# Attention block on one core: the durations and latencies in the kernel's own planner are replaced, and the first key mask is computed ahead of an evacuation

## The chip, the core and the metric

The kernel runs on one core of a Trainium2 chip. The metric is the device time of one execution in microseconds, the median of three runs. Five engines take part, each with its own instruction queue, worked off in order: PE (TensorE, matmuls), ACT (ScalarE), DVE (VectorE), POOL (GpSimd) and SP (SyncE, which here only issues DMAs).

## The reference

The inputs are x of 1 x 2048 x 448, wqkv of 448 x 1344 and wo of 448 x 448, all bf16. There are 16 heads of width 28.

```
qkv = (x @ wqkv).reshape(B, S, 3, H, Dh).transpose(2, 0, 3, 1, 4)
q, k, v = qkv[0], qkv[1], qkv[2]
scores = einsum("bhqd,bhkd->bhqk", q, k) * (Dh ** -0.5)
p = softmax(scores, axis=-1)
o = einsum("bhqk,bhkd->bhqd", p, v)
return o.transpose(0, 2, 1, 3).reshape(B, S, D) @ wo
```

## The kernel before, in words

**Tiles.** The 16 heads are four groups of four heads, the 2048 queries four column blocks of 512, and the 2048 keys 16 rows of 128. A window is one group with one block of queries: 16 windows, each with 16 rows of keys times four heads, 64 score tiles of 128 keys x 512 queries. The first two windows are cut: their rows 0 to 3 come first, then the other rows of each.

**What happens to a score tile.** A score tile is one matmul of KB (keys) and QB (queries) into PSUM (L868, `emit_S`). The extra rows in KB and QB carry an upper bound of the score, so that the exponential cannot overflow: NK (L580 for the first group, L619 for the others) is the key side of this bound, made from the maximum of the absolute keys (KPART, KMAX), and SP copies it into KB with DMAs (L595, L617). The keys themselves are evacuated from PSUM into KB (L544, L553, L561) and moved between KB's partitions by DMAs (L585, L607). From the score tile the exponential is taken in one of three ways:

- ACT: two tiles lie side by side in one of the two PSUM tiles PA, and one ACTIVATE Exp of 128 x 1024 writes PTA (L1291).
- DVE with GpSimd: the tile lies in one of three PSUM banks PD. DVE computes DU from it (L1072), then DV from it and DU (L1075); GpSimd multiplies the two into DG (L1078); DVE adds it to the tile in PSUM and writes PTD (L1091), which frees the bank. So a tile takes three passes of DVE and one of GpSimd.
- GpSimd alone: DVE copies the tile from PD to SG (L1004), and GpSimd does six operations (L1011 to L1034) that end in PTD.

When all four heads of a row are there, four matmuls add the row to PO (L1136). After a window's last row DVE copies PO to OSB (L939 and L953 for the cut windows, L956), the sums go through DRAM and come back as reciprocals, GpSimd multiplies (L971), and after the last group the output projection follows (L792, L810). In PE's spare time stand the projections for Q (L656), K (L525) and V (L727) of the next group and, where nothing else is to be done, matmuls of zeros that keep PE active (L1252).

**What sets the order.** Each operation is an `Op` with an engine, a duration, a latency until another may use its result, its needs, a due time and conditions. The planner at the end of the kernel's function (L1327 to L1396) runs through time as it believes it to pass, and at each moment gives a free engine an operation that is ready by its belief: `try_static` for DVE, POOL and SP takes the one with the earliest due time; `try_pe` prefers a score pair for PA, then looks at static work, score tiles for PD, PO rows and fillers; `try_act` takes the exponentials as they come. Which tile goes which way is decided here too: a tile goes to PD when a bank is free in the planner's time. What comes out is a fixed order of instructions for each engine. On the chip each engine follows it and waits on semaphores for what it needs. So a constant in the planner is not a duration on the chip; it moves instructions in the queues, and it changes how many tiles each engine gets.

The names that the change touches: MM (a matmul), MODE (what a change between score, PO and filler matmuls costs), SLAT, PLAT (latencies of PE's results), P1, CPY, EVK, RED (DVE passes), PTT, PTS, PST (GpSimd), SEM (the latency that an `Op` has if none is given, 0.13), PFIN, PGAP, PLD (GpSimd's hand-overs), ASL, ELAT (end of an exponential), SLK and MG (margins), and the numbers J0, J1, J3, JL, O1, O2, OF, RV, LA, GY, GS, UK, UQ, UO for how many rows PO waits for and how far ahead each kind of work is due.

Of the kernel before, what the change touches and what calls it, by code (L numbers as in the profile page):

```python
# [39 lines left out]

SEM = 0.13
MM = 0.22
MODE = 0.105
PLAT = 0.24
P1 = 0.598
TT5 = 0.33
TS5 = 0.2
PTT = 1.12
PTS = 0.59
PST = 1.125  # L50
CPY = 0.6
EVK = 0.66
RED = 0.59
# [29 lines left out]
def kernel(  # L83
# [31 lines left out]
    UK = 30  # L115
# [3 lines left out]
    LA = 10  # L119
# [3 lines left out]
    GY = 0.5  # L123
    GS = 1.0
    GBEG = 40
    J0 = 10
    NTAIL = 8
    JL = 6
    JACC = 8
    DI = 1  # L130
    PVM = 0.0
    PLD = 0.2
    YIELD = 0
    SLAT = 0.5
    ASL = -0.05
    ELAT = 0.05
    PGAP = 0.03
    PFIN = 0.3
# [5 lines left out]
    J3 = 9  # L144
    UQ = 60
    OD = 2
    PADQ = 1
    O1 = 10
    O2 = 20
    OF = 0.4  # L150
    RV = 2
    QPR = 100
    LOOK = 0.2
    SLK = 0.13
    MG = 0.1
# [7 lines left out]
    UO = 40  # L163
    FB = TPC
    NF = 2
    J1 = 8
# [189 lines left out]

    def step():
        pos[0] += 1
        while pos[0] in taken:
            pos[0] += 1  # L360
# [125 lines left out]
    k0mv = []  # L486
    m0 = Op("DVE", 0.0, None)
# [23 lines left out]
    def task_K(g, sc):  # L511
        due = g * 4 * WT - 200 + 36 * sc
        if g == 0:
            task = {"slot": None, "ap": k0_bank[sc]}
            acq = lambda t: all(o.done(t) for o in k0_wait[sc]())
            elig = None
            prio = -1000 + 10 * sc + 15 if sc else -4560
        else:
            task = bank_task()
            acq = acq_d(task, urgent=(g - 1) * 4 * WT + (sc + 1) * KSP - UK)  # L520
            elig = at((g - 1) * 4 * WT + sc * KSP + 2)
            prio = due
# [8 lines left out]
        if g == 0:  # L531
# [18 lines left out]
            else:  # L550
# [6 lines left out]
                evs[0].acq = lambda t: red.start is None or red.done(t)  # L557
# [13 lines left out]
    def task_kmax(g):  # L571
# [7 lines left out]
        if g == 0:  # L579
            nk = add(Op("DVE", 0.2, lambda: nc.vector.tensor_scalar(  # L580
                out=NK[0][:], in0=maskm[:, 0:P], scalar1=KMAX[0][:, 0:1], scalar2=RK0[:, 0:1], op0=ALU.mult, op1=ALU.mult),
                deps=[m] + rk_op, prio=prio + 0.2))
            for n, (c0, c1) in enumerate(KCH):
                for i in range(HG):
# [3 lines left out]
                        deps=[k0ev[sc] for sc in range(c0, c1)], prio=-2000 + 20 * n + i, lat=DLAT + 0.3))  # L588
# [8 lines left out]
            for n, (c0, c1) in enumerate(RCH):  # L597
                for i in range(HG):
                    o = add(Op("SP", DISS + 0.07, (lambda i=i, c0=c0, c1=c1: rep0(i, c0, c1)), deps=[nk],
                               prio=(-1990 + 20 * n if c0 else -300) + 0.1 * i, lat=DLAT + 0.6, elig=None if c0 else lambda t: pos[0] >= NF * FB * HG + 4))  # L600
                    for c in range(c0, c1):
                        kmrep[(g, c, i)] = o
# [28 lines left out]
    def task_Q(g, c):  # L631
# [9 lines left out]
        else:  # L641
            task = bank_task()
            acq = acq_d(task, urgent=w * WT - UQ)
            elig = at((w - 1) * WT + 3 - (QEA if w > 3 else 0))
            prio = due - (QPR if w > 3 else 0)
# [71 lines left out]
    def task_V(g, jq):  # L717
        due = g * 4 * WT + jq * TPC * HG - 12 + (FB * HG * (NF - 1) if g == 0 and jq else 0)
        task = bank_task()
        early = False  # L720
        elig = at(VE + jq * 5 if g == 0 else (g - 1) * 4 * WT + jq * WT + 4)
# [8 lines left out]
        for jj in range(TPC):  # L730
            ops.append(add(Op("PE", 0.27, (lambda jj=jj: mm(jj)), deps=(xt_done[jq] + [wvin]) if jj == 0 else [ops[-1]],
                              prio=prio + 0.001 * jj, kind="W", elig=elig, acq=acq_d(task, early, urgent=due - UV if g == 0 else (g - 1) * 4 * WT + (jq + 1) * WT + 32) if jj == 0 else None,
                              lat=0.0 if jj < TPC - 1 else PLAT)))
# [9 lines left out]
        ev = add(Op(eng, 0.54, ev_fn, deps=[ops[-1]], prio=prio - (0 if early else 1000), elig=elig))  # L743
# [43 lines left out]
    def task_part(c, n):  # L787
        due = (12 + c) * WT - PARTD
        for tq in n:
# [4 lines left out]
                [ot_done[(g, c)] for g in range(G - 1)], due + tq * 10, at(12 * WT - PARTE), acq_d(task, urgent=due + PARTU))  # L794
# [5 lines left out]
    def task_OP(c):  # L800
        due = (12 + c + 1) * WT + 16
        st = add(Op("SP", 0.05, None, prio=due))
        evs = []
        for tq in range(TPC):
            if c == NQC - 2 and tq == ATQ:
# [6 lines left out]
                [ot_done[(g, c)] for g in range(g0, G)], due + tq * 10, None, acq_d(task, urgent=NT - UO))  # L812
# [125 lines left out]
    def finish_block(w, pvop):  # L938
        ev = add(Op("DVE", 0.62, lambda: nc.vector.tensor_copy(out=OSB[w][:], in_=PO[:]), deps=[pvop], prio=-5000))  # L939
# [7 lines left out]
    def finish_window(w, pvop):  # L947
# [4 lines left out]
        if w < NF:  # L952
            ev = add(Op("DVE", 0.62, lambda: nc.vector.tensor_tensor(out=OSB[b][:], in0=PO[:], in1=OSB[b][:], op=ALU.add),  # L953
                        deps=[pvop] + first_part[w], prio=-5000))
        else:
            ev = add(Op("DVE", 0.62, lambda: nc.vector.tensor_copy(out=OSB[b][:], in_=PO[:]), deps=[pvop] + ([prev] if prev else []),  # L956
                        prio=-5000))

        def rel(t):
# [12 lines left out]
                    deps=o4, prio=-10, kind="n"))  # L972
# [17 lines left out]
    def quiet(t):  # L990
        for o in static["DVE"]:
            if o.kind == "sb" and (o.elig is None or o.elig(t)) and all(d.end is not None and d.end <= t + GS for d in o.deps):
                return False
        return not any(o.kind == "p" and o.deps[0].end is not None and o.deps[0].end + o.deps[0].lat < t + GY for o in static["POOL"])

    def start_g(n, sop, slot, sg):
# [7 lines left out]
        cp = add(Op("DVE", CPY, lambda: nc.vector.tensor_copy(out=X[:], in_=PX[slot.idx][:]), deps=[sop], prio=n - O1))  # L1004
# [21 lines left out]
        def acq(t):  # L1026
# [8 lines left out]
            out=PTD[st["s"].idx][:].bitcast(U16), in0=X[:], scalar1=1.0, scalar2=EBITS + CK0, op0=ALU.mult, op1=ALU.add), deps=[g5], prio=prio + 5, kind="g", elig=quiet, acq=acq, lat=PFIN))  # L1035
# [15 lines left out]
    def ahead(t):  # L1051
# [3 lines left out]
        for k in range(k0 + LA, k0 + LA + LAR):  # L1055
# [7 lines left out]
    def start_tile(n, sop, slot, early):  # L1063
        if early:
# [9 lines left out]
            deps=[sop] + prevl, prio=n - O1))  # L1074
        p2 = add(Op("DVE", P1, lambda: nc.vector.scalar_tensor_tensor(  # L1075
            out=DV[b][:], in0=lo, scalar=65536 * (SS - 0.5 + CE / C3), in1=DU[b][:], op0=ALU.add, op1=ALU.mult),
            deps=[p1], prio=n - O2, lat=0.22))
# [5 lines left out]
        def acq(t):  # L1083
# [9 lines left out]
            op0=ALU.add, op1=ALU.add), deps=[gq], prio=n - OF, acq=acq))  # L1093
# [81 lines left out]

    def try_pe(t):

        late = MODE if last_fam[0] == "S" else 0.0
# [288 lines left out]
```

## Time and profile before

| | |
|---|---|
| time, median of three runs (from 408.28 to 408.6) | 408.47 us |
| time of the profiled execution | 408.52 us |
| its span, first to last instruction | 406.7 us |
| exponentials on ACT, tiles through DVE and GpSimd, tiles through GpSimd alone | 421, 158, 24 |
| first exponential starts, last one ends | 11.02 us, 398.91 us |
| GpSimd's multiplication for DG (L1078), mean | 1154 ns |
| GpSimd's six operations for one tile (L1011 to L1034), means | 617, 618, 1156, 1154, 1154, 618 ns |
| PE waits for an exponential to free PA | 35.6 us, 107 times |
| granted TensorE clock, mean | 0.999 |

The profile is of one execution. Its page gives each engine's busy time, the chain of work that ended last, and groups of instructions by source line: busy time in total, mean duration of one, and the engine's idle time just before them with what ended it. Durations of neighbours on an engine can overlap, so that the distance from one start to the next is shorter than the duration. The timeline gives start and duration of each instruction; where several of a line follow each other it puts them in one row with a count. Times in the timeline count from the start of the span.

### The profile page before, as it was taken

How to read it: one execution, taken by the hardware profiler on the slowest of the kernel's cores; microseconds unless marked ns; L12 is line 12 of the kernel's file. 1: busy time of each engine (PE TensorE's matmuls, PEld its weight loads, DVE VectorE, ACT ScalarE, POOL GpSimd, SP SyncE). 2: the span in 40 equal slices, each digit the busy share in tenths (PEclk: the TensorE clock that was granted, in tenths of full speed). 3: DMA queues.
4: the chain of work that ended last, by engine and by line, in shares of the span. 5: the costliest groups of instructions: out<-in, count | busy, mean ns of one | idle time of the engine just before them, and what ended most of it. 6: DMA issues, size and time to landing. Idle time of an engine off the chain costs nothing.

```text
span 406.7 us, 7593 instructions
## 1 busy us (share of the span) xinstructions
PE 362.2 (89%) x2606; PEld 121.4 (30%) x2606; DVE 381.5 (94%) x671; ACT 393.6 (97%) x432; POOL 331.5 (82%) x357
## 2 busy tenths in 40 slices
PE   8999888898998989899898989899898888989896
PEld 5243232323222222222323223232322222222232
DVE  6998999999999999989999998999989999999995
ACT  4989999999999999999999999999999999999994
POOL 4038799678699899998989898898898889999860
PEclk9999999999999999999999999999999999999999
DMA  9351130211400002100510000010130101000112
GB/s 219 44 86 39 48 76 3 50 27 28 96 5 27 19 24 35 16 25 6 110 30 27 23 4 26 2 47 21 48 59 15 35 1 46 22 20 10 47 73 90
DMA packets 36446, 16.58 MB, mean 41 GB/s; under 512 B 28784, under 2 KB 33136, under 8 KB 36408
## 3 DMA queue, kind: packets, MB, share of 16 engines
q1 hardware_dynamic: 35800, 15.89, 16.7%
q8 instruction: 20, 0.33, 0.3%
q10 hardware_dynamic: 608, 0.22, 0.2%
q14 instruction: 18, 0.15, 0.1%
HBM read 7.44 MB, written 1.97 MB: 23 GB/s over the span
## 4 chain that ended last, share of the span: by engine, by line
ACT 74%; PE 16%; issue 7%; DVE 1%; ACTq 0%
ACT PTA L1291 74%; PE PA L868 6%; PE PO L1136 4%; PE PD L868 1%; PE PD L810 1%; PE PA L396 1%; PE PO L810 1%; PE PD L417 1%; DVE DU L1072 0%; DVE DV L1075 0%; PE PO L525 0%; PE PD L525 0%; PE PA L417 0%; PE PD L902 0%; PE PD L656 0%
## 5 line engine op out<-in xcount | busy, mean ns | idle before, releaser
L1291 ACT ACTIVATE PTA<-PA 128x1024 bf16<-128x1024 f32 x421 | 386.6, 1222 | 1.3 <-PE PA L868 1.3
L1078 POOL TENSOR_TENSOR DG<-DV,DU 128x512 f16<-128x512 f16 x158 | 180.7, 1154 | 46.6 <-DVE DV L1075 36.5
L868 PE MATMUL PA<-QB,KB 64*128 64x512 bf16 x842 | 167.4, 380 | 38.2 <-ACT PTA L1291 35.6
L868 PEld LDWEIGHTS <-KB 64*128 64x128 bf16 x1024 | 67.6, 93 | 181.8 <-issue 174.1
L1072 DVE TENSOR_SCALAR DU<-PD 128x512 f16<-128x512 uint16 x158 | 104.9, 680 | 7.3 <-PE PD L868 6.8
L1091 DVE SCALAR_TENSOR_TENSOR PTD<-PD,DG 128x512 uint16<-128x512 f32 x158 | 106.5, 679 | 3.6 <-POOL DG L1078 2.7
L1075 DVE SCALAR_TENSOR_TENSOR DV<-PD,DU 128x512 f16<-128x512 uint16 x158 | 105.5, 681 | 1.0
L1136 PE MATMUL PO<-PTA,VA 128*32 128x512 bf16 x842 | 86.1, 386 | 0.0
L868 PE MATMUL PD<-QB,KB 64*128 64x512 bf16 x182 | 65.2, 377 | 0.6
L1136 PE MATMUL PO<-PTD,VA 128*32 128x512 bf16 x182 | 52.2, 387 | 0.0
L1136 PEld LDWEIGHTS <-VA 128*32 128x32 bf16 x1024 | 19.0, 94 | 47.6 <-issue 47.4
L1021 POOL TENSOR_TENSOR SG<-SG,GU 128x512 f32<-128x512 f32 x24 | 27.7, 1154 | 1.4 <-DVE QP L695 0.4
L1017 POOL TENSOR_TENSOR GV<-GE,GU 128x512 f16<-128x512 f32 x24 | 27.8, 1156 | 1.2
L1019 POOL TENSOR_TENSOR GU<-GV,GU 128x512 f16<-128x512 f16 x24 | 27.7, 1154 | 0.4
L971 POOL TENSOR_TENSOR OT<-OSB,RRB 128x512 bf16<-128x512 f32 x15 | 19.0, 1270 | 3.2 <-DVE DU L1072 2.4
L1011 POOL TENSOR_SCALAR GU<-SG 128x512 f16<-128x512 uint16 x24 | 14.8, 617 | 6.6 <-DVE SG L1004 3.0
L656 PE MATMUL PO<-XT,WQP 112*128 112x512 bf16 x56 | 18.7, 386 | 0.0
L1004 DVE COPY SG<-PD 128x512 f32<-128x512 f32 x24 | 16.4, 682 | 1.8 <-PE PD L868 1.8
L1014 POOL TENSOR_SCALAR GE<-SG 128x512 f32<-128x512 uint16 x24 | 14.8, 618 | 3.3 <-DVE QP L695 1.8
L525 PE MATMUL PO<-XT,WKP 112*128 112x512 bf16 x52 | 16.9, 385 | 0.0
L727 PEld LDWEIGHTS <-XT 112*128 112x128 bf16 x256 | 13.5, 98 | 10.5 <-issue 10.3
L1034 POOL TENSOR_SCALAR PTD<-SG 128x512 uint16<-128x512 f32 x24 | 14.8, 618 | 1.0
(108 smaller groups left out, 193.7 us busy)
## 6 DMA issues: line engine op xcount, KB each, us to landing
RRB<-SCR SPq DMA_DIRECT2D x15, 256.0 KB
QB<-QP SPq DMA_DIRECT2D x56, 32.0 KB
KB<-NK SPq DMA_DIRECT2D x12, 128.0 KB
XS<-in_x_dram SPq DMA_DIRECT2D x3, 448.0 KB
QB<-QB SPq DMA_DIRECT2D x28, 32.0 KB
out_dram<-XS SPq DMA_DIRECT2D x2, 448.0 KB
KB<-KB SPq DMA_DIRECT2D x6, 128.0 KB
RRB<-SCRF SPq DMA_DIRECT2D x2, 256.0 KB
```

Of the source, the lines that this page charges most:

```text
L656: ops = chain_mm(CC, lambda cc: nc.tensor.matmul(out=ap(), lhsT=WQP[g][:, cc, :], rhs=XT[c][cc // 2][0:CK, cc % 2, :], start=(cc == 0), st ...
L868: nc.tensor.matmul(out=ap, lhsT=KB[g % 2][i // 2][a:a + 64, j * P:(j + 1) * P], rhs=QB[w % NQB][i // 2][a:a + 64, :], start=True, stop=Tru ...
L971: o5 = add(Op("POOL", 1.22, lambda: nc.gpsimd.tensor_tensor(out=OT[g][c][:], in0=OSB[b][:], in1=RRB[b][:], op=ALU.mult), deps=o4, prio=-10 ...
L1017: g3 = add(Op("POOL", PTT, lambda: nc.gpsimd.tensor_tensor(out=GV[:], in0=GE[:], in1=GU[:], op=ALU.mult), deps=[g2], prio=prio + 2, kind=" ...
L1019: g4 = add(Op("POOL", PTT, lambda: nc.gpsimd.tensor_tensor(out=GU[:], in0=GV[:], in1=GU[:], op=ALU.mult), deps=[g3], prio=prio + 3, kind=" ...
L1021: g5 = add(Op("POOL", PST, lambda: nc.gpsimd.tensor_tensor(out=X[:], in0=X[:], in1=GU[:], op=ALU.add), deps=[g4], prio=prio + 4, kind="g", ...
L1072: p1 = add(Op("DVE", P1, lambda: nc.vector.tensor_scalar(out=DU[b][:], in0=lo, scalar1=SIG / 65536, scalar2=SIG * (SS - 0.5), op0=ALU.mult ...
L1075: p2 = add(Op("DVE", P1, lambda: nc.vector.scalar_tensor_tensor(out=DV[b][:], in0=lo, scalar=65536 * (SS - 0.5 + CE / C3), in1=DU[b][:], o ...
L1078: gq = add(Op("POOL", PTT, lambda: nc.gpsimd.tensor_tensor(out=DG[b][:], in0=DV[b][:], in1=DU[b][:], op=ALU.mult), deps=[p2], prio=n, kind ...
L1091: f = add(Op("DVE", P1, lambda: nc.vector.scalar_tensor_tensor(out=PTD[st["s"].idx][:].bitcast(U16), in0=PX[slot.idx][:], scalar=EBITS + C ...
L1136: nc.tensor.matmul(out=PO[HP * st:HP * (st + 1), :], lhsT=VA[g][:, j, st, :], rhs=r["p"][i][1](), start=first, stop=last, tile_position=(0 ...
L1291: nc.scalar.activation(out=PTA[pslot.idx][:, 0:len(ns) * QW], in_=PA[s.idx][:, 0:len(ns) * QW], func=ACT.Exp, bias=ACT_BIAS, scale=ACT_SCALE)
```

## The change

The durations of the planner's operations are replaced: DVE, GpSimd and the matmul by slightly shorter ones, and MODE by a table PACE with a distance for each pair of kinds of matmul (S a score pair, s a single score tile, V a PO row, F a filler). GpSimd's latency at the end of an operation goes from 0.3 to 0.075 (0.2 at the end of a tile that is GpSimd's alone), with 0.12 more where one operation of such a tile follows another. PE may go further past the end of an exponential (SLK). DU gets no latency and the copy to SG 0.165. An operation counts as ready as soon as one that it needs on the same engine has ended. In the first group the last evacuation of keys (L553 in before) may only come after the reduction of its block and after NK, if that reduction has begun; and the DMAs that move keys of rows 8 to 15 come after the first four DMAs of the mask. The numbers for how far ahead work is due move into a table PLAN with one entry for each window; its values are the numbers of before. All else in the diff is the new names' use.

Below is the diff, cut to its core.

```diff
@@ -38,19 +38,47 @@
+PLAN = {
+    "PVROWS": [8, 10, 10, 10, 10, 10, 10, 10, 10, 10, 10, 10, 9, 9, 9, 6],
+    "AHEAD": [10, 10, 10, 10, 10, 10, 10, 10, 10, 10, 10, 10, 10, 10, 10, 10],
...
+    "TAIL": [8, 8, 40, 1],
...
+}
+
 SEM = 0.13
-MM = 0.22
-MODE = 0.105
-PLAT = 0.24
+MM = 0.2
+PACE = {"SS": 0.43, "Ss": 0.215, "SV": 0.32, "SF": 0.324, "sS": 0.262, "ss": 0.22, "sV": 0.303, "sF": 0.306,
+        "VS": 0.345, "Vs": 0.332, "VV": 0.226, "VF": 0.33, "FS": 0.37, "Fs": 0.31, "FV": 0.31, "FF": 0.207}
+TDEP = 0.12
+PLAT = 0.21
 P1 = 0.598
 TT5 = 0.33
-TS5 = 0.2
-PTT = 1.12
-PTS = 0.59
-PST = 1.125
-CPY = 0.6
-EVK = 0.66
-RED = 0.59
+TS5 = 0.198
+PTT = 1.108
+PTS = 0.582
+PST = 1.108
+CPY = 0.598
+EVK = 0.657
+RED = 0.57
...
-    PLD = 0.2
+    PLD = 0.16
     YIELD = 0
-    SLAT = 0.5
-    ASL = -0.05
-    ELAT = 0.05
-    PGAP = 0.03
-    PFIN = 0.3
+    SLAT = 0.39
+    ASL = 0.051
+    ELAT = 0.06
+    PGAP = 0.0
+    PFIN = 0.075
...
-    SLK = 0.13
-    MG = 0.1
+    SLK = 0.24
+    MG = 0.0
...
-                evs[0].acq = lambda t: red.start is None or red.done(t)
+                evs[0].acq = lambda t: (red.start is None or red.done(t)) and (sc < NQC - 1 or red.start is None or (nk0 and nk0[0].start is not None))
...
-                        deps=[k0ev[sc] for sc in range(c0, c1)], prio=-2000 + 20 * n + i, lat=DLAT + 0.3))
+                        deps=[k0ev[sc] for sc in range(c0, c1)], prio=-2000 + 20 * n + i, lat=DLAT + 0.3,
+                        elig=(lambda t: all(r.start is not None for r in rep0s[0:HG])) if n else None))
...
-        cp = add(Op("DVE", CPY, lambda: nc.vector.tensor_copy(out=X[:], in_=PX[slot.idx][:]), deps=[sop], prio=n - O1))
+        cp = add(Op("DVE", CPY, lambda: nc.vector.tensor_copy(out=X[:], in_=PX[slot.idx][:]), deps=[sop], prio=n - PLAN["LEADC"][now()], lat=0.165))
...
             out=DU[b][:], in0=lo, scalar1=SIG / 65536, scalar2=SIG * (SS - 0.5), op0=ALU.mult, op1=ALU.add),
-            deps=[sop] + prevl, prio=n - O1))
+            deps=[sop] + prevl, prio=n - PLAN["LEAD1"][now()], lat=0.0))
         p2 = add(Op("DVE", P1, lambda: nc.vector.scalar_tensor_tensor(
             out=DV[b][:], in0=lo, scalar=65536 * (SS - 0.5 + CE / C3), in1=DU[b][:], op0=ALU.add, op1=ALU.mult),
-            deps=[p1], prio=n - O2, lat=0.22))
+            deps=[p1], prio=n - PLAN["LEAD2"][now()], lat=0.157))
...
+    pe_last = [0.0]
+
+    def pe_at(t, fam):
+        return max(t, pe_last[0] + PACE[last_fam[0] + fam])
+
     def try_pe(t):
 
-        late = MODE if last_fam[0] == "S" else 0.0
         for s in a_slots:
-            if s.free_at + late <= t + 1e-9 and pos[0] < NT and s_ready(pos[0], t) and s_ready(after(pos[0]), t):
+            if s.free_at <= pe_at(t, "S") + 1e-9 and pos[0] < NT and s_ready(pos[0], t) and s_ready(after(pos[0]), t):
...
         def fits(dur, fam):
-            d = dur + (MODE if fam != last_fam[0] else 0.0) + (MODE if fam != "S" else 0.0)
-            return not tight or not any(t < x and t + d > x + SLK for x in exp_ends)
+            u = pe_at(t, fam) + PACE[fam + "S"]
+            return not tight or not any(t < x and u > x + SLK for x in exp_ends)
...
-            if all(d.done(t) for d in o.deps) and (o.acq is None or o.acq(t)):
+            if all(d.done(t) or d.eng == e and d.end is not None and d.end <= t + 1e-9 for d in o.deps) and (o.acq is None or o.acq(t)):
...
                 if e == "PE":
-                    fam = {"s": "S", "B": "F", "W": "F", "K": "F", "A": "F", "T": "F"}.get(o.kind, o.kind)
-                    if fam != last_fam[0]:
-                        o.dur += MODE
+                    fam = {"B": "F", "W": "F", "K": "F", "A": "F", "T": "F"}.get(o.kind, o.kind)
+                    x = pe_at(t, fam)
+                    pe_last[0] = x + o.dur - MM
+                    o.dur += x - t
...
                 if e == "POOL":
+                    if o.kind == "g" and (pool_last[0] in o.deps or o.dur == PTS and o.deps[0].eng == "DVE"):
+                        o.dur += TDEP
+                    pool_last[0] = o
```

## The prediction, made before the changed kernel was run

> **What bounds the kernel now.** I read the page's table of engines, then the chain, then the groups of instructions, and went into the trace for the spacing of instructions.
>
> ```profile
> PE 362.2 (89%) x2606; PEld 121.4 (30%) x2606; DVE 381.5 (94%) x671; ACT 393.6 (97%) x432; POOL 331.5 (82%) x357
> ...
> ACT 74%; PE 16%; issue 7%; DVE 1%; ACTq 0%
> ...
> L1291 ACT ACTIVATE PTA<-PA 128x1024 bf16<-128x1024 f32 x421 | 386.6, 1222 | 1.3 <-PE PA L868 1.3
> ...
> L1072 DVE TENSOR_SCALAR DU<-PD 128x512 f16<-128x512 uint16 x158 | 104.9, 680 | 7.3 <-PE PD L868 6.8
> ```
>
> ACT is busy 97%, and 74% of the chain is its exponentials. There are 421, each busy 1222 ns, but overlapped: from the first start (11.02) to the last (397.65) they follow each other every 0.92 us, and only 13 of the 420 distances are over 0.947. What those 13 have above 0.917 is 4.0 us together, and 1.4 of it is one place, after the 15th exponential:
>
> ```profile
> 20.98 3.90 ACT L1291 ACTIVATE PTA<-PA 128x1024 bf16<-128x1024 f32 x4
> 25.44 1.02 ACT L1291 ACTIVATE PTA<-PA 128x1024 bf16<-128x1024 f32 x1 [0.56 <-PE PA L868]
> 26.93 1.02 ACT L1291 ACTIVATE PTA<-PA 128x1024 bf16<-128x1024 f32 x1 [0.47 <-PE PA L868]
> ```
>
> So a better order alone can win 4 us at most; more only with fewer exponentials on ACT. DVE is the next engine, and its 94% is no share of its room: passes overlap too. The timeline of DVE shows its two rates (columns: start, duration):
>
> ```profile
> 203.04 0.68 DVE L1091 SCALAR_TENSOR_TENSOR PTD<-PD,DG 128x512 uint16<-128x512 f32 x1
> 203.63 0.68 DVE L1075 SCALAR_TENSOR_TENSOR DV<-PD,DU 128x512 f16<-128x512 uint16 x1
> 204.23 0.68 DVE L1004 COPY SG<-PD 128x512 f32<-128x512 f32 x1
> 204.83 0.68 DVE L1072 TENSOR_SCALAR DU<-PD 128x512 f16<-128x512 uint16 x1
> 205.54 0.69 DVE L1075 SCALAR_TENSOR_TENSOR DV<-PD,DU 128x512 f16<-128x512 uint16 x1
> 206.15 0.68 DVE L1091 SCALAR_TENSOR_TENSOR PTD<-PD,DG 128x512 uint16<-128x512 f32 x1
> ```
>
> A pass that does not read the result of the one before it starts 0.60 after it (203.04, 203.63, 204.23, 204.83). A DV right behind the DU that it reads starts 0.71 after it (204.83, 205.54): it waits for the end of the 0.68. In before, 29 DUs stand directly ahead of their own DV, and all 29 distances are 0.711 to 0.726 (median 0.714); other passes have a median of 0.598. One such hand-over costs **0.116 us**.
>
> **The change, part by part.** The constants themselves cost nothing on the chip; they move the order that the planner writes out. I counted instructions and neighbours in the built order of both kernels.
>
> *Tiles between engines.* Exponentials 421 to 419: ACT is 2 x 0.9126 (310.3 us of the stage below by its 340 exponentials) = 1.8 us shorter. Tiles on the DVE/GpSimd path 158 to 164: 18 more DVE passes. Tiles on GpSimd alone 24 to 22: two copies (L1004) less. DVE: (18 - 2) x 0.598 = **+9.6 us**. GpSimd: 6 x 1.154 - 2 x (3 x 1.154 + 3 x 0.618) = -3.7 of 331.5: nothing, for it has 75 us idle; were it bound, this would be a gain.
>
> *Hand-overs on DVE.* The diff lets the planner start an operation at the very end of one that it needs on the same engine, and gives DU no latency (0.13 before), so DU-DV in a row is planned at 2 x 0.598. It now puts **142** DUs of 164 right ahead of their own DV (29 before). QB-QP goes from 1 to 7 such pairs, KB-KPART from 0 to 5, QP-QP from 0 to 2, NK after KMAX from 0 to 1. That is 128 more over the whole run: 128 x 0.116 = **+14.8 us** of DVE which the plan does not hold.
>
> From DVE's first reduction (7.8) to the transpose that closes the last window (399.6), its instructions at their undisturbed spacing, hand-overs included, sum to 370.5 in before: 21.3 idle. The same sum over the after order is 394.9. The added 24.4 are more than all the idle time.
>
> The middle, window by window, decides. From the copy of the 4th PO result (68.83 in the trace; L953/L956 make one per window or part) to the 17th (379.07) are 310.3 us, and ACT has no gap over 0.32 there:
> - DVE before: 398 passes x 0.598 + 21 copies x 0.598 + 93 other operations (42.9) + 27 x 0.116 = 296.6.
> - DVE after: 417 x 0.598 + 18 x 0.598 + 91 others (41.6) + 132 x 0.116 (15.3) = **317.1**.
> - ACT: 338 exponentials before; 335 after, x 0.9126 = 305.7.
>
> DVE passes ACT by 11.4 us, and in each of the 13 windows, so no window repays another. What is late next: a late PTD holds the PO matmuls that read it, a late PTD keeps its PD bank, and both stand in PE's queue ahead of the score matmuls for PA, so ACT gets gaps.
>
> On top comes the idle time that DVE keeps:
>
> ```profile
> DVE DU L1072 <- PE PD L868: 6.8, 14, 1.1
> DVE PTD L1091 <- POOL DG L1078: 2.7, 5, 0.7
> DVE SG L1004 <- PE PD L868: 1.8, 5, 0.8
> ```
>
> These 11.3 us are waits for engines that will be early when DVE is late. From below 0; from above the whole idle of the stage, 310.3 - 296.6 = 13.7. I take a third of 11.3, **3.8**: in 27 places of the after order a DU follows the PTD that frees its bank with at most one pass between, and that trip through PE stays.
>
> *The first key mask.* In before DVE does this:
>
> ```profile
> 20.18 0.16 DVE L575 TENSOR_REDUCE KMAX<-KPART 128x1 f32<-128x4 f32 x1
> 20.25 0.74 DVE L553 TENSOR_SCALAR KB<-PO,onescol 128x512 bf16<-128x512 f32 x1
> 20.91 0.30 DVE L580 TENSOR_SCALAR NK<-maskm,KMAX,RK 128x128 bf16<-128x128 bf16 x1
> ```
>
> NK moves ahead of the KB evacuation: 0.66 earlier. But two other things change. The second reduction now stands ahead of the first of these KB evacuations, 0.6 later for it, and SP issues that one's four KB moves (0.63 each, 18.32 to 20.84) ahead of the mask. The first mask DMA went out at 21.63; SP gets to it at 21.1 to 21.5 now. Worth 0.1 to 0.5; ends 0 and the 1.4 idle of those two exponentials; I take 0.3. The four moves for rows 8 to 15 go behind the mask; before, three of the four went there as well (24.35 to 26.2), and their rows are some 12 exponentials away: nothing, and 0.6 (one issue) if that cover were short. The mask's later part and the Q moves stay behind them in SP's queue in the same sequence.
>
> *PE.* 30 more keep-warm matmuls x 0.227 = 6.8 us, in time in which PE waits for ACT anyway (35.6 us, 107 times); with that cover gone they would cost those 6.8. Two fillers instead of one between the first score pairs: K of the last column block is ready about 0.8 earlier (counted above). Of GpSimd's instructions 329 carry a wait, 331 before: nothing.
>
> **The sum.** 4th copy: by ACT two more exponentials lie ahead of it, 68.8 + 1.8 - 0.3 = 70.3; by DVE 7.8 + 62.1 (its sum up to there, 56.3 before) + 1.2 (two waits for PE, 0.6 each, before 25 us) = 71.1. I take 71.0. Then 317.1 + 3.8. From the 17th copy to the end took 406.7 - 379.1 = 27.6 with 21 exponentials to go; 20 now: 26.7. Together 418.6 of span. The profiled execution took 408.52 for its span of 406.7, so 1.8 lie around it, and it is 0.05 from the median of 408.47: **420.4 us**, +2.9%.
>
> One rule speaks against this. The Trainium skill, "VectorE: DVE Perf Modes", section "The DRAIN you can't avoid", reports eight copies in the same 13.88 us with a semaphore after each or only after the last, and says that the semaphore costs nothing extra there. By that the hand-overs would be free, DVE's stage 301.8, and ACT would stay the bound. The 29 distances of this trace say otherwise for a pass that reads its predecessor's result, and I go by them.
>
> **Rivals.**
> - *ACT stays the bound (faster).* Place: the 132 hand-overs of the middle. Were their price nearly nothing in the new order, DVE's stage would be 317.1 - 15.3 = 301.8, under ACT's 305.7, and the time 408.5 - 1.8 - 0.3 = 406.4; with all of the early gap gone 405.3. It decides from a price under about 0.03 us (301.8 + 132 x 0.03 = 305.7). Against it: no hand-over in before is under 0.11. Also here: the change does what it says. I put the time at 406.
> - *The idle time swallows the load (same).* If the 17th copy came only as late as the fewer exponentials after it allow, 408 to 409. Against: it needs DVE's sum to be 10 us too high.
> - *DVE is the bound and keeps its idle time.* The order was written for another pace, so DVE goes on waiting for PE and GpSimd as now: 71.0 + 317.1 + 13.7 + 26.7 + 1.8 = 430.3. For it: the queues are fixed, and a late engine delays the engines that it waits for. Against: in before ACT, the bound, loses only 1.7 us in that stage.
>
> **Chances.** Forecast (414 to 426) 0.74; ACT the bound 0.08; same 0.03; idle kept (over 426) 0.15. The low end takes no idle time, 416.6, and lets the last PTDs of a window stand four passes (2.4 us) ahead of its copy: 414. For the high end I go to 428.5, short of 430.3 (about 0.08 left out above it). A measurement of this kernel tells about 0.2% (0.8 us) from no change: faster 0.08, within 0.03, slower 0.89.
>
> **What would show it.** After: about 419 exponentials with mean distance 0.94 or more in the middle, gaps spread over the windows and released by PE; DVE's DU to DV distance 0.71 in 142 places; DVE's idle before DU and PTD under 6 us; PE waiting for DVE instead of ACT in front of PA; GpSimd's idle larger. Wrong if the exponentials stand at 0.913 throughout, or if DV starts 0.60 behind its DU. If the gaps sit in a few places with DVE idle, the order and not the load is the cause.

## The result and the profile after

The changed kernel takes 436.07 us (median of four runs, 433.72 to 438.4), the kernel before in the same set 408.46: a ratio of **1.068, 95% interval 1.061 to 1.074**. The prediction said slower, 420.4 us with a range of 414 to 428.5; the direction holds, the size does not. Against the median the forecast is 15.7 us short. The profiled execution is the slowest of the four: it took 438.4, its span is 436.3, and the prediction's sum for the span was 418.6. So in this execution **17.7 us** are to be explained.

First the page of the changed kernel, the rows that answer to those shown of before: engines, the granted TensorE clock in 40 slices (all 9 in before), the chain, and the groups of the exponential and of DU.

```profile
PE 368.3 (84%) x2617; PEld 114.5 (26%) x2636; DVE 401.7 (92%) x687; ACT 401.3 (92%) x430; POOL 330.0 (76%) x351
...
PEclk9899889989999999999989999999999979999999
...
DVE 68%; PE 13%; DMA 6%; POOL 5%; issue 4%; ACT 2%; SPq 1%; DVEq 0%; POOLq 0%; ACTq 0%
...
L1318 ACT ACTIVATE PTA<-PA 128x1024 bf16<-128x1024 f32 x419 | 394.2, 1045 | 23.1 <-PE PA L891 19.3
...
L1095 DVE TENSOR_SCALAR DU<-PD 128x512 f16<-128x512 uint16 x164 | 111.6, 681 | 6.3 <-PE PD L891 6.1
```

The chain has gone from ACT to DVE, as predicted. But two things were not: DMA has 6% of the chain, and the clock row has dips. The mean of one exponential even fell, from 1222 to 1045 ns, for a reason that costs time: fewer of them overlap with a neighbour (one that starts after an idle ACT takes 1.02 us, as at 53.69 below).

The timeline of DVE shows the hand-over at the predicted price: DU at 203.40, its DV 0.71 later, while the PTD at 202.20 starts 0.61 after a DV.

```profile
201.59 0.69 DVE L1098 SCALAR_TENSOR_TENSOR DV<-PD,DU 128x512 f16<-128x512 uint16 x1
202.20 1.28 DVE L1114 SCALAR_TENSOR_TENSOR PTD<-PD,DG 128x512 uint16<-128x512 f32 x2
203.40 0.68 DVE L1095 TENSOR_SCALAR DU<-PD 128x512 f16<-128x512 uint16 x1
204.11 0.69 DVE L1098 SCALAR_TENSOR_TENSOR DV<-PD,DU 128x512 f16<-128x512 uint16 x1
```

All 142 distances lie at 0.663 to 0.727, median 0.715. The exponentials now have a mean distance of 0.9955; 113 distances are over 0.947, and what these have above 0.917 is 35.2 us (before: 13 and 4.0). About half of the 35.2 is spread in gaps of 0.03 to 0.8, which is what a loaded DVE gives. The other half, some 17 us, sits in five places: 14 to 17, 49 to 57, 93 to 97, 221 to 228 and 345 to 353. The timeline of the second, all engines, read from top to bottom:

```profile
38.78 0.67 SPq L956 DMA_DIRECT2D SCRF<-RR  x1
...
40.59 1.21 SPq L957 DMA_DIRECT2D RRB<-SCRF  x2
...
49.44 1.26 POOL L967 TENSOR_TENSOR OSB<-OSB,RRB 128x512 f32<-128x512 f32 x1 [1.50 <-DMA RRB<-SCRF]
...
51.84 0.69 DVE L1114 SCALAR_TENSOR_TENSOR PTD<-PD,DG 128x512 uint16<-128x512 f32 x1 [3.48 <-POOL DG L1101]
...
52.59 0.58 PE L891 MATMUL PD<-QB,KB 64*128 64x512 bf16 x1 [3.53 <-DVE PTD L1114]
...
53.69 1.02 ACT L1318 ACTIVATE PTA<-PA 128x1024 bf16<-128x1024 f32 x1 [3.53 <-PE PA L891]
```

SP issues the write SCRF<-RR at 38.78 in 0.67 us, and the read RRB<-SCRF, which needs its data, can follow only at 40.59, when the write has landed. The read's second half lands at 49.3; GpSimd waits for it (2.28 us for the first half, 1.50 for the second), its DG behind it comes late, so DVE's PTD waits 3.48, PE 3.53 for the PD bank, and ACT 3.53 for PE. No engine is overloaded here: one late DMA goes through four queues. From 51.10, still within the stall, PE runs at half its clock for 6.83 us. The kernel before has the same pair at the same distance, 1.80 us, and no wait behind it:

```profile
36.72 0.67 SPq L933 DMA_DIRECT2D SCRF<-RR  x1
38.52 1.21 SPq L934 DMA_DIRECT2D RRB<-SCRF  x2
...
47.01 2.49 POOL L944 TENSOR_TENSOR OSB<-OSB,RRB 128x512 f32<-128x512 f32 x2
```

So the pair itself is not what is new. In the changed kernel it goes out 2.1 us later, and GpSimd's queue is at the multiplication by 44.39 (46.67 less the wait of 2.28), not at 47.01. The code says why it is there early: in the plan the write has a latency of 2.0 us, and the new readiness rule leaves it out for an operation on the same engine, so the plan takes the read, and its data, to come 2 us sooner than before.

SP's own waits show that late DMAs are no single case. First before, then the changed kernel:

```profile
SPq L968 <- DMA SCR<-DRC: 10.2, 7, 3.2
...
SPq L710 <- DMA QB<-QB: 1.4, 1, 1.4
```

```profile
SPq L991 <- DMA SCR<-DRC: 21.1, 15, 2.7
SPq L733 <- DMA QB<-QB: 15.3, 13, 3.3
```

Over all its lines SP waits 41.8 us for DMAs to land, 17.7 in before; for the compute engines the rows of waits for DMAs add up to 21.1 us (3.9 before).

### The profile page after: what moved, and what is told of

It is laid out like the page before. It is cut to its first block, busy times and chain, and to the rows that moved or that the text cites. A ratio compares the mean times of both kernels' runs of the same rounds, so it can differ in the third digit from the quotient of the medians.

```text
span 436.3 us, 7621 instructions
## 1 busy us (share of the span) xinstructions
PE 368.3 (84%) x2617; PEld 114.5 (26%) x2636; DVE 401.7 (92%) x687; ACT 401.3 (92%) x430; POOL 330.0 (76%) x351
## 3 DMA queue, kind: packets, MB, share of 16 engines
q1 hardware_dynamic: 35800, 15.89, 15.7%
## 4 chain that ended last, share of the span: by engine, by line
DVE 68%; PE 13%; DMA 6%; POOL 5%; issue 4%; ACT 2%; SPq 1%; DVEq 0%; POOLq 0%; ACTq 0%
DVE DV L1098 20%; DVE DU L1095 18%; DVE PTD L1114 17%; PE PA L891 4%; POOL DG L1101 3%; PE PO L1159 3%; DMA RRB<-SCRF 2%; DVE SG L1027 2%; DVE QB L689 2%; DVE VA L765 2%; PE PD L891 2%; ACT PTA L1318 2%; DVE KB L581 1%; DVE OSB L979 1%; DMA RRB<-SCR 1%
## 5 line engine op out<-in xcount | busy, mean ns | idle before, releaser
L1318 ACT ACTIVATE PTA<-PA 128x1024 bf16<-128x1024 f32 x419 | 394.2, 1045 | 23.1 <-PE PA L891 19.3
L1101 POOL TENSOR_TENSOR DG<-DV,DU 128x512 f16<-128x512 f16 x164 | 188.4, 1153 | 66.9 <-DVE DV L1098 64.3
L891 PE MATMUL PA<-QB,KB 64*128 64x512 bf16 x838 | 181.5, 391 | 25.0 <-ACT PTA L1318 21.7
L1098 DVE SCALAR_TENSOR_TENSOR DV<-PD,DU 128x512 f16<-128x512 uint16 x164 | 113.1, 690 | 4.9
L1095 DVE TENSOR_SCALAR DU<-PD 128x512 f16<-128x512 uint16 x164 | 111.6, 681 | 6.3 <-PE PD L891 6.1
L891 PEld LDWEIGHTS <-KB 64*128 64x128 bf16 x1024 | 54.9, 93 | 191.4 <-issue 177.3
L891 PE MATMUL PD<-QB,KB 64*128 64x512 bf16 x186 | 69.8, 384 | 27.7 <-DVE PTD L1114 20.3
L1044 POOL TENSOR_TENSOR SG<-SG,GU 128x512 f32<-128x512 f32 x22 | 25.4, 1156 | 3.2 <-DVE QP L718 2.4
L1040 POOL TENSOR_TENSOR GV<-GE,GU 128x512 f16<-128x512 f32 x22 | 25.4, 1157 | 1.6 <-DVE QP L718 0.6
L1042 POOL TENSOR_TENSOR GU<-GV,GU 128x512 f16<-128x512 f16 x22 | 25.4, 1153 | 0.4
L1279 PE MATMUL PO<-zrow,zeros 128*128 128x512 bf16 x49 | 17.8, 391 | 2.0 <-issue 1.4
L750 PEld LDWEIGHTS <-XT 112*128 112x128 bf16 x256 | 13.9, 97 | 11.5 <-issue 11.3
L545 PE MATMUL PO<-XT,WKP 112*128 112x512 bf16 x52 | 15.9, 383 | 0.4
```

What stands on the lines that cost most here:

```text
L891: nc.tensor.matmul(out=ap, lhsT=KB[g % 2][i // 2][a:a + 64, j * P:(j + 1) * P], rhs=QB[w % NQB][i // 2][a:a + 64, :], start=True, stop=Tru ...
L1040: g3 = add(Op("POOL", PTT, lambda: nc.gpsimd.tensor_tensor(out=GV[:], in0=GE[:], in1=GU[:], op=ALU.mult), deps=[g2], prio=prio + 2, kind=" ...
L1042: g4 = add(Op("POOL", PTT, lambda: nc.gpsimd.tensor_tensor(out=GU[:], in0=GV[:], in1=GU[:], op=ALU.mult), deps=[g3], prio=prio + 3, kind=" ...
L1044: g5 = add(Op("POOL", PST, lambda: nc.gpsimd.tensor_tensor(out=X[:], in0=X[:], in1=GU[:], op=ALU.add), deps=[g4], prio=prio + 4, kind="g", ...
L1095: p1 = add(Op("DVE", P1, lambda: nc.vector.tensor_scalar(out=DU[b][:], in0=lo, scalar1=SIG / 65536, scalar2=SIG * (SS - 0.5), op0=ALU.mult ...
L1101: gq = add(Op("POOL", PTT, lambda: nc.gpsimd.tensor_tensor(out=DG[b][:], in0=DV[b][:], in1=DU[b][:], op=ALU.mult), deps=[p2], prio=n, kind ...
```

## The experiments

| kernel | median us | ratio to before, 95% interval | hand-overs on DVE |
|---|---|---|---|
| changed kernel | 436.07 | 1.068 (1.061 to 1.074) | 164 |
| 1 no reread | 425.74 | 1.042 (1.037 to 1.047) | 23 |
| 2 two lines put back | 410.71 | 1.006 (1.004 to 1.008) | 30 |
| 3 the two lines alone | 429.46 | 1.053 (1.048 to 1.059) | 159 |
| 4 hand-overs priced | 422.13 | 1.034 (1.032 to 1.035) | 150 |
| 5 old rule for SP | 424.56 | 1.040 (1.039 to 1.042) | 163 |
| 6 new rule for SP alone | 424.55 | 1.039 (1.036 to 1.042) | 38 |
| 7 as 5, no reread | 410.71 | 1.007 (1.005 to 1.009) | 26 |
| 8 as 5, priced | 410.33 | 1.004 (1.003 to 1.006) | 151 |
| 9 SP re-sorted only | 428.12 | 1.049 (1.047 to 1.050) | 164 |
| 10 mask alone | 413.13 | 1.013 (1.010 to 1.015) | 43 |
| 11 other constants alone | 408.27 | 1.000 (0.999 to 1.001) | 31 |
| 12 as 11, old slack, priced | 411.34 | 1.010 (1.007 to 1.012) | 21 |
| 13 mask by hand on before | 408.52 | 1.000 (0.999 to 1.001) | 37 |
| 14 mask by hand on 11 | 408.75 | 1.001 (1.001 to 1.002) | 32 |
| 15 change less mask | 436.63 | 1.068 (1.067 to 1.070) | 164 |

A hand-over is a DVE pass directly behind the one whose result it reads. **Theory A** was the prediction's own: hand-overs that the plan does not hold overload DVE, and that alone. **Theory B**: the new constants for PE make a worse order.

### Hand-overs, and the two lines that make them (1 to 4)

1, in the changed kernel's order; DV no longer rereads the DU written just before it, which leaves the values of these tiles wrong:

```diff
-            out=DV[b][:], in0=lo, ..., in1=DU[b][:], op0=ALU.add, op1=ALU.mult),
+            out=DV[b][:], in0=lo, ..., in1=DU[(b - 1) % NB if k else b][:], op0=ALU.add, op1=ALU.mult),
```

> The changed kernel with its order kept on every engine; only DV reads the DU of the tile before instead of its own (this leaves the exponential of these tiles wrong), so DV no longer waits for the instruction ahead of it. Hand-overs on DVE 164 to 23. Theory A (the unplanned hand-overs overload DVE, and all else follows from its lag): DU to DV 0.60, ACT the bound again, 405 to 410 us, the granted clock at most once halved, in the head. Rival B (the new PE distances and margins make an order with idle PE, late DMAs and a halved clock; the hand-overs are only their own 16 us): 418 us or more, the clock still halved in the middle.

2, in the changed kernel; 3 is the reverse of it in the kernel before:

```diff
-            deps=[sop] + prevl, prio=n - PLAN["LEAD1"][now()], lat=0.0))
+            deps=[sop] + prevl, prio=n - PLAN["LEAD1"][now()]))
...
-            if all(d.done(t) or d.eng == e and d.end is not None and d.end <= t + 1e-9 for d in o.deps) and (o.acq is None or o.acq(t)):
+            if all(d.done(t) for d in o.deps) and (o.acq is None or o.acq(t)):
```

> The changed kernel with two lines put back: DU has its latency again, and a need on the same engine counts as ready only after the latency. All measured durations, the PE table, the margins and the mask stay. 420 exponentials, 161 and 24 tiles, 30 hand-overs. Theory A: 405 to 411 us, as fast as before or a little faster. Rival B: 425 us or more, for all that it blames is still there.

> The kernel before with only these two lines changed (DU without latency, a need on the same engine ready at its end). 421 exponentials, 160 and 23 tiles, 159 hand-overs. DVE has 123 x 0.116 = 14.3 us more of hand-overs and 3 us more of passes, against 21.3 us idle. Theory A: 418 to 438 us, DVE on the chain, the clock halved in places. Rival B: 408 to 412 us.

4, in the changed kernel:

```diff
+    dve_last = [None]
...
+                if e == "DVE":
+                    if dve_last[0] in o.deps:
+                        o.dur += 0.116
+                    dve_last[0] = o
```

> The changed kernel, but the planner adds 0.116 to a DVE operation when the one ahead of it on DVE is among its needs. The order keeps 150 hand-overs, 422 exponentials, 157 and 23 tiles. Theory A: it is not the hand-overs but that the plan does not hold them, 406 to 412 us. Rival B: 425 us or more. If hand-overs hurt by themselves even when planned: 413 to 420 us.

2 and 3 show that nearly the whole loss hangs on these two lines: without them 410.71, with them alone on the kernel before 429.46. But 1 and 4 say that hand-overs are not all of it. 1 has few of them and the changed kernel's order, and still takes 425.74, which lies in rival B's band; the gaps that are left (24.9 us) stand in a few places, the largest 4.2 us at 47, 2.4 at 335 and 1.6 at 214, again with PE and GpSimd waiting for DMAs. 4 has its hand-overs in the plan and takes 422.13, which lies in none of its three bands. Theory A falls as the only cause, and theory B with it, since 2 keeps all of PE's constants.

That led to **theory C**: the new readiness rule ("an operation counts as ready as soon as one that it needs on the same engine has ended") holds for every engine, SP too. On SP an operation "ends" when the DMA is issued. So the plan puts a DMA that needs another DMA's data right behind it. That can cost time in two forms: SP's queue stops there until the data has landed, and all DMAs behind go out late; and the engines' own order is made for data that is not there yet, as in the stall at 49.

### Hand-overs and SP's queue, one at a time (5 to 8)

5, in the changed kernel; 6 has `e == "SP"` in that place and DU's old latency; 7 is 5 with the edit of 1, 8 is 5 with the edit of 4:

```diff
-            if all(d.done(t) or d.eng == e and d.end is not None and d.end <= t + 1e-9 for d in o.deps) and (o.acq is None or o.acq(t)):
+            if all(d.done(t) or e != "SP" and d.eng == e and d.end is not None and d.end <= t + 1e-9 for d in o.deps) and (o.acq is None or o.acq(t)):
```

> Edit: the changed kernel, but SyncE (SP) alone keeps the old rule, so a DMA that needs an earlier DMA is planned behind that one's landing and not at the end of its issue. The order has 418 exponentials, 167 + 21 tiles on the DVE path and on GpSimd alone, 163 hand-overs between neighbours on DVE (138 of them DU to DV). Theory C (two causes: unplanned hand-overs on DVE, and an SP queue planned without the landing of its DMAs, each worth 10 to 15 us, with the halved TensorE clock behind the stalls of the second): 416 to 424 us, no GpSimd or TensorE wait of over 1 us on a DMA in the middle, few or no stretches of halved clock. Theory A (hand-overs alone): 430 to 438. Theory B (TensorE's constants alone): 430 to 438.

> Edit: the opposite of the one before: of the changed kernel, the new rule is left to SP alone, and DU keeps the old latency of 0.13 in the plan. 420 exponentials, 161 + 23 tiles, 38 hand-overs on DVE. Theory C: 418 to 424 us (410.7 of the kernel without either, and 8 to 14 for SP), with waits of GpSimd and TensorE on DMAs and stretches of halved clock behind them. Theory A: 409 to 412, since the hand-overs are gone.

> Edit: as the first of this set (SP keeps the old rule), and DV reads the DU of the tile before in place of its own, so that the same order has 26 hand-overs in place of 163. The exponentials of the DVE tiles are wrong by that. Theory C: both causes are gone, 405 to 411 us, and 9 to 14 less than the first of this set; exponentials at about 0.92. Theory B (TensorE's constants or the order for their sake cost time too): over 414.

> Edit: as the first of this set (SP keeps the old rule), and the plan adds 0.116 us to a DVE operation that stands right behind one that it needs. 422 exponentials, 158 + 23 tiles, 151 hand-overs, all of them in the plan. Theory C: 407 to 413 us, 9 to 15 less than the same with SP under the new rule (422.13). Theory A in the form that hand-overs cost the same planned or not: 418 to 424. Theory B: over 418.

With 2 these make a square: neither cause 410.71, hand-overs alone (5) 424.56, SP alone (6) 424.55, both 436.07. So each is worth **13.8 to 13.9 us** alone, and the two together 25.4: they add up but for 2.3 us. Only 5 and 7 share one order, so only that 13.85 is free of a change of plan. 6 and 2 are plans of their own, and plans without either cause differ by up to 4.9 us (2, 8, 10, 11 and 12 lie from 408.27 to 413.13); SP's 13.8 is uncertain by about as much, and that the two numbers agree so well may be chance. 5 and 6 came out just above theory C's bands (by 0.6), 7 and 8 inside; theory A's numbers for 5, 6 and 8 all fail.

The two causes look different in the profile. In 5, first, the chain is DVE's and the gaps (21.9 us, 100 of them) are spread but for one of 2.7 at 88 (a gap of over 1 us near that place stands in 2, 7, 10 and 12 too, with the mask part and without it; 4 and 8 have none), no engine has a wait of over 1 us for a DMA in the middle, and the clock is whole. In 6, second (waits), DVE has room, but PE and through it ACT wait for single DMAs:

```profile
DVE 80%; PE 8%; POOL 4%; DMA 3%; issue 3%; SPq 1%; ACT 1%; DVEq 0%; POOLq 0%
```

```profile
ACT PTA L1318 <- PE PA L891: 13.4, 11, 4.0
...
PEld L891 <- DMA KB<-NK: 6.9, 5, 2.9
```

8 shows that hand-overs need not be avoided if they are planned. It has 151 of them and 158 DVE tiles, and takes 410.33 to 5's 424.56; its page:

```profile
DVE 46%; ACT 27%; PE 16%; issue 6%; POOL 4%; DMA 0%; SPq 0%; DVEq 0%; POOLq 0%
...
L1318 ACT ACTIVATE PTA<-PA 128x1024 bf16<-128x1024 f32 x422 | 388.0, 1106 | 1.2 <-PE PA L891 1.0
```

ACT's idle before an exponential is 1.2 us, as in before (1.3): told of the price, the planner gives DVE nine tiles less than in 5 and GpSimd alone two more. That is 27 DVE passes less and two copies more, 25 x 0.598 = 15.0 us by the prediction's price of a pass, against the 14.2 gained: the hand-overs still cost DVE their time, and the planner makes room for it.

### Only SP's queue (9)

5 and 6 are new plans, in which everything moves. 9 keeps the changed kernel's order on PE, ACT, DVE and GpSimd, and re-sorts SP's entries alone:

```diff
+    log[:] = [(max([t] + [d.end + d.lat for d in o.deps if d.eng == "SP"]) if o.eng == "SP" else t, q, o) for t, q, o in log]
     log.sort(key=lambda e: (e[0], e[1]))
```

> Edit: the changed kernel with its own order on TensorE, ScalarE, VectorE and GpSimd, instruction for instruction; only SyncE's queue is re-sorted, so that a DMA that needs an earlier DMA stands where the plan has that one landed, and what can go before goes before. 164 hand-overs as in the changed kernel. Theory C in its form 'the blocked queue' (DMAs behind the blocked one go out late, and the engines find them missing): 424 to 429 us, the waits on DMAs gone and no halved clock. Theory C in its form 'the plan counts on data that is not there' (the engines' own order is too early for it): 431 to 437, the waits on DMAs remain. Theory A: 433 to 438.

428.12: inside the band for the blocked queue, 8.0 us gained without touching a compute engine's order. SP's waits for DMAs fall from 41.8 to 16.1:

```profile
SPq L991 <- DMA SCR<-DRC: 7.7, 6, 2.6
SPq L640 <- DMA KB<-KB: 5.0, 4, 3.5
```

The stall at 49 shrinks to 1.1 us: the read goes out at 36.90, 3.7 us earlier, and still GpSimd waits 1.46 for it. The waits of the compute engines for DMAs fall from 21.1 to 11.9 and not to nothing, and a stretch of halved clock is left at 216, so the other form of the theory (the plan also counts on data before it is there) has a share too. How large it is can't be told from this run alone; by the square both forms together take 436.07 - 424.56 = 11.5 from the changed kernel, with the uncertainty of a new plan.

### The mask and the rest (10 to 15)

10 is the kernel before with the mask part of the diff alone. 11 is the changed kernel with the edit of 2 and without the mask part; 12 is 11 with SLK back at 0.13 and the edit of 4. 15 is the changed kernel without the mask part.

> Edit: the kernel before with the mask part of the change alone: NK ahead of the last KB evacuation, and the K moves of rows 8 to 15 behind the first mask's DMAs. 421 exponentials as before; 157 + 26 tiles for 158 + 24; 43 hand-overs for 36. Prediction's step: 0.1 to 0.5 us gained from the gap at the 15th exponential (1.4 us there before), so 407.9 to 408.4, less 0.1 if the seven hand-overs count; first mask DMA out at 21.1 to 21.5. Rival (the mask's gain is hidden or the new order gives it back): 408.4 to 410.

> Edit: the changed kernel without the mask part, and with the old same-engine rule and DU's old latency, so that what is left are the new constants of TensorE, GpSimd and the DMAs. 420 exponentials, 161 + 23 tiles, 31 hand-overs. Theory C: 409 to 411 us (410.7 of the same with the mask part), so that the other constants cost 1 to 2 us through small gaps; the mask part is worth within 0.5 either way. If the mask is what costs the 2 us: 408 to 409.

> Edit: as the kernel with the other constants alone, and two more: TensorE's matmuls may run past an exponential's end by 0.13 again (0.24 in the changed kernel), and hand-overs on DVE are planned at their 0.116. 420 exponentials, 160 + 24 tiles, 21 hand-overs. If TensorE's longer slack makes the small gaps (44 over 0.03 us with it, 13 in the kernel before): 407.4 to 408.6, under the kernel before by the one exponential (0.9); if not: 409 to 411.

10 missed by far: 413.13 where both sides gave at most 410. The gap at the 15th exponential is gone, as the step hoped. But the plan made anew behind it is worse: at 88.5 there is a gap of 3.9, in which PE works for 3.5 us on PO rows and V without a score pair, while the Q moves for the next window run from 87.04 to 92.0 (78.45 to 87.2 in before); and from 52.36 to 69.43 the clock is halved. 11 shows that all the other constants together are worth nothing (420 exponentials, 408.27; theory C gave 409 or more, the mask as the cause 408 to 409), and 2, which has the mask part besides, is 2.4 slower. 12 missed too. It changes the slack and the price of hand-overs at once and has fewer small gaps than 11 (26 for 43), but three of over 1 us where 11 has one, and takes 3.1 more. So it does not settle what the slack is worth; and since 12 has no mask part, a new plan can lose as much at 85 to 89 us without it.

Was it the earlier mask or the new plan? 13 and 14 put the mask into a fixed order by hand, in before and in 11; the engines but DVE (one swap) and SP (one move of K) keep their order:

```diff
+    ev0 = max((o for o in k0ev.values() if o.eng == "DVE" and o.start < nk0[0].start), key=lambda o: o.start)
+    by_hand = {id(nk0[0]): ev0.start - 1e-7}
+    for n, o in enumerate(k0mv[HG:]):
+        if o.start < rep0s[HG - 1].start:
+            by_hand[id(o)] = rep0s[HG - 1].start + 1e-7 * (n + 1)
```

> Edit: the kernel before, its order kept instruction for instruction on TensorE, ScalarE and GpSimd; by hand NK goes ahead of the last KB evacuation on VectorE, and on SyncE one K move of rows 8 to 15 goes behind the first mask's DMAs. If the earlier mask is worth what the prediction's step says: 0.1 to 0.7 us gained, 407.7 to 408.3, first mask DMA 0.6 earlier against the first K move. If the earlier mask itself costs time (K late for rows 8 to 15): 409 to 413.

> Edit: the same by hand in the order of the kernel with the other constants alone (408.27). If the earlier mask is worth what the step says: 407.5 to 408.2; with all of the gap of 1.1 at that place 407.2. If the earlier mask itself costs time: 409 to 411.

> Edit: the changed kernel without the mask part. 419 exponentials, 164 + 22 tiles, 164 hand-overs, as in the changed kernel; so the two causes, hand-overs and SyncE's queue, are all there. If the mask part costs here what it costs in the other plans (2.4 to 4.7): 431 to 434. If its worth is lost among the stalls: 435 to 438.

In 13 the first mask DMA goes out 2.62 after the first K move, 3.31 in before: 0.69 earlier, as the step had it (0.66). And the time is the same within 0.1%. The gap at the 15th exponential stands as it was; the timeline of 13, of PE and then of ACT, shows why:

```profile
23.28 0.77 PE L731 MATMUL PD<-WV,XT 112*128 112x112 bf16 x12
23.98 0.62 PE L1140 MATMUL PO<-PTA,VA 128*32 128x512 bf16 x8
24.52 0.41 PE L872 MATMUL PA<-QB,KB 64*128 64x512 bf16 x2
24.92 0.55 PE L731 MATMUL PD<-WV,XT 112*128 112x112 bf16 x8
25.52 0.59 PE L660 MATMUL PO<-XT,WQP 112*128 112x512 bf16 x2
26.04 0.60 PE L872 MATMUL PA<-QB,KB 64*128 64x512 bf16 x4
```

```profile
24.97 1.02 ACT L1295 ACTIVATE PTA<-PA 128x1024 bf16<-128x1024 f32 x1 [0.56 <-PE PA L872]
26.47 3.77 ACT L1295 ACTIVATE PTA<-PA 128x1024 bf16<-128x1024 f32 x4 [0.47 <-PE PA L872]
```

PE does not wait for keys there. It works through V, PO and Q matmuls that stand ahead of the score pairs. So in a fixed order an earlier mask is worth nothing (13 and 14 lie between the bands of both sides); 10's loss is the new plan. Made anew, a plan does use it: the distances after the 15th and 16th exponential hold together 1.42 us above 0.917 in before, 1.54 in 11 and 1.73 in 12, where the mask is late; 0.35 in 10, 0.89 in 2 and 0.48 in the changed kernel, where it is early; and 1.42 in 13 and 1.56 in 14, early in the old order.

15 tells nothing of the mask. Its trace has the changed kernel's instructions in the changed kernel's order on every engine, at the mask too: with the new readiness rule NK stands ahead of the last evacuation and the later K moves behind the mask without the mask part (in 3 as well). So 15 is the changed kernel once more, 436.63 to 436.07. None of the runs beats the kernel before by more than 0.2%; 11 equals it.

## Why the prediction was wrong, by its own steps

- **Which engine bounds: right.** DVE takes over, 68% of the chain, and ACT is down to 2%. A slip beside it: the 0.9126 for one exponential divides the stage by 340, and it holds 338 by the text's own list; with 0.918 ACT's sum is 307.5, not 305.7, still under DVE's 317.1.
- **Hand-overs: right in price and count.** 142 DU-DV pairs at 0.715. Between 5 and 7, the same order but for what DV reads, 137 hand-overs less are worth 13.85 us, 0.101 each. That is less than 137 x 0.116 = 15.9, since in 7 DVE is only 39% of the chain and not all that it saves shows; the term of 128 x 0.116 = 14.8 stands. What it left out: a DV right behind its DU also holds the next pass for 0.608 in place of 0.598 (medians, 142 and 22 places; 0.598 in 7, where DV reads another DU), some 1.4 us in all. The rule that the prediction weighed against its rows (a semaphore costs nothing extra there) does not carry over to a pass that reads the result of the one before.
- **The tail: right, with some luck.** 17th copy to the end 26.7 us, as predicted, but with 19 exponentials in it and not the 20 that the step counted.
- **The start of the middle: wrong by 7.7.** The 4th copy came at 78.7, not 71.0. The stall at 49 with its halved clock is 5.2 of that, gaps in the head at 14 to 17 are 1.4. Both sums for this step counted instructions and took DMAs to land when they are needed.
- **The idle time that DVE keeps: the step that failed in size, 13.8 in place of 3.8.** From the 4th to the 17th copy took 330.9, the prediction's DVE sum is 317.1. The places at 93, 221 and 345 hold 3.1 + 3.3 + 3.9 = 10.3 us of ACT's gaps, and in each the engines wait for DMAs: Q's moves at 93 and 345 (up to 1.9 us), the mask's at 221 (1.3). Its 13.7 for the upper bound was the idle of before; what came is a new kind of idle, which that bound could not hold. With SP re-sorted (9) the 4th copy is at 73.3, the stage takes 325.1 and the tail 26.4: 2.3 and 4.2 over the forecast in place of 7.7 and 10.
- **Where it went wrong in the reading.** The step on the readiness rule says that the planner may start an operation at the very end of one that it needs on the same engine, and then counts pairs on DVE alone. The mask step says that the later moves stay in SP's queue "in the same sequence"; it looked at the sequence around the mask, not at how far apart a DMA stands from the one that it needs. The wait of a DMA for a DMA stood in the sum at nothing, without a reason. Read for all engines the rule was the second half of the loss: 8.0 us come back when SP's queue alone is re-sorted (9), and some 13.8 stand between the plans with the rule for SP and without (6 against 2).
- **PE: costed at nothing, and its clock not looked at.** Stalls of 1.0 to 3.5 us on PE are followed by stretches at half clock. After the stall at 49 the next gaps, 1.03 and 0.53, are of that kind.
- **The mask: 0.3 gained, right at its place, not shown in the time.** In a fixed order it is worth nothing (13, 14), since PE is at work on matmuls that the plan has put there. In a new plan the gap shrinks, in the changed kernel from 1.42 to 0.48 (0.79 in 15, the same kernel), but the plans with it lose 2.4 (2 against 11) and 4.7 (10) elsewhere. That the mask and not the mere change of plan costs this is not shown: 12 loses 3.1 without it.
- **What would show it.** Mean distance, 142 pairs and GpSimd's idle (106 us, 75 before) came as written. PE waits 20.3 us for DVE's PTD, but still 21.7 for ACT. DVE's idle before DU and PTD is 12.7, not under 6, and half of the gaps sit in few places: the text's own sign that the order, not the load, is a cause. Its range left out the rival that belonged to that sign.

## What to carry to other kernels

When a scheduler's rule changes, go through every queue that it governs, and the DMA queue first: there the end of an instruction is not the arrival of its data (0.67 us to issue the write above, 1.8 until the read could follow), and an in-order queue hands the wait to everything behind. A term for a bottleneck engine's load and a term for late data need separate looks, since here the first spread small gaps and the second made few large ones. A gap beside an event is not simply a wait for it: see what the engine does in the gap, and whether the order will be made anew, before pricing its removal. And where a planner makes every order anew, compare causes in a fixed order: plans without either cause differed here by up to 4.9 us.

## What the runs showed of the hardware

The granted TensorE clock falls to 0.5 for 3.41 us or a multiple: in the changed kernel from 51.10 (6.83), 95.47 (3.41), 225.18 (3.41) and 348.06 (6.83), in 10 from 52.36 (17.07). The starts lie on one grid (95.47 - 51.10 = 44.37 = 13 x 3.413). The windows view, for PE, of the 3.41 us ahead of each start in the changed kernel (length, busy time, matmuls, clock, and the DMA engines' share and GB/s):

```profile
47.69:51.10 3.41, 1.36 (x17) 1.00 0.08 29
92.06:95.47 3.41, 1.85 (x18) 1.00 0.19 48
221.77:225.18 3.41, 2.22 (x14) 1.00 0.60 114
344.65:348.06 3.41, 1.31 (x13) 1.00 0.08 20
```

PE is busy 38 to 65% in them; in before no such window of the middle is under 74%. In kernel 10:

```profile
48.95:52.36 3.41, 2.13 (x10) 1.00 0.21 67
52.36:55.77 3.41, 3.04 (x10) 0.50 0.29 25
```

62% busy, and half the clock follows, though PE had no idle time of over 0.6 us there, only several of 0.1 to 0.5. Over the traces of all sixteen kernels and of before, on this grid, from 10 us on and ahead of the tail, among windows at the full clock: every one under 57% was followed by half the clock; of those between 59 and 68% some were and some were not; above that it happened twice, in the head of the changed kernel (13.55, after 82%) and in kernel 14 (56.08, after 79%). What decides between 59 and 68%, and these two, is left open. Once halved, the clock often stayed so after a busier window (10 stays at half for 17.07 us with windows of 89% and more). The Trainium skill, "TensorE: Matmul & The Clock Gate", section "Part 1: The HAM clock gate (the "warmup" mystery)", gives a free-running window of 3413 ns, which agrees with the grid. Its subsection "HAM oscillation — how this bites in real kernels" puts the danger at PE-idle gaps of over some 3.4 us, and here gaps of 1.0 to 1.9 (ahead of 95.47, 225.18 and 348.06), or many short ones, were enough.

The other unexpected thing is how far a plan carries a small edit: one DVE instruction and one DMA moved by hand cost nothing (13), and the same edit given to the planner cost 4.7 us (10), through places 30 to 70 us later.
